# Where three convolution units stand among the matrix products of a fused convolution and feed-forward kernel

## The chip, the cores and the metric

The kernel runs on one core of a Trainium2 chip. The metric is the device time of one execution in microseconds (us); a number of executions is summed up by their median. The core has five engines that run side by side: TensorE (PE; the loads of its stationary operands are listed as PEld), VectorE (DVE), ScalarE (ACT), GpSimd (POOL) and SyncE (SP), which here only issues transfers. Matmul results go to PSUM, a small memory from which VectorE and ScalarE read them.

## The reference

The input x has 8 sequences of 3904 rows with 192 columns. A causal convolution with 7 taps runs along each sequence; the taps are a softmax of the weights, and each of 8 heads (24 columns) has its own. The result goes through a product of two linear maps and two more linear maps:

```python
w = weight - np.max(weight, axis=-1, keepdims=True)
w = np.exp(w)
w = w / (np.sum(w, axis=-1, keepdims=True) + 1e-09)
...
out = np.einsum('hk,bskhg->bshg', w, x_unf)
...
a = x @ w1
b = x @ w2
h = a * b @ w3
return (h @ w_out).astype(np.float32)
```

w1 and w2 are 192 x 1024, w3 is 1024 x 1024, w_out 1024 x 192. The output has 31232 rows of 192 numbers.

## The kernel before

The 31232 rows are cut into two streams of 15616 (`NS`, index `r`), and each stream into 31 chunks of up to 512 rows (`R`). w3 and w_out are multiplied once, early, to one matrix `W_sb` of 1024 x 192, so that per chunk two products are left:

- `first_product(R)` (L581) computes a and b for both streams. For each of 8 blocks of 128 columns (`ft`) PE writes two PSUM tiles, `pa` and `pb`, with 12 matmuls in all, which use the array in halves of 64 rows. ACT casts `pa` to `asb` (L603), DVE multiplies `asb` by `pb` and writes the result to `abT` (L605). The text calls the tiles of ft 6 pa6 and pb6, those of ft 7 pa7 and pb7.
- `second_product(R, r)` (L615) multiplies `abT` by `W_sb` with 32 matmuls on the whole array (L621) into one PSUM tile `ops`; ACT copies it out (L626), SP stores it.

All PSUM tiles come from one pool with four buffers of two banks each (`banks`, L97, L98): each new tile takes the buffer of the tile four before it, whatever its name, and its first write waits until the reader of that older tile is done.

The convolution is done in two ways. For some chunks ("side", L49) it is a sum over taps: ACT makes the first product (`side_first`, L494), DVE adds five more and a last one (`side_sums`, L512), and POOL does some by itself (L539, L559). For the other chunks it is done on PE: `conv` (L310) multiplies rows of x by a small banded matrix `Aband`, with tiles of 32 x 32 of the array. It is called in **units**: one unit is `conv` for two heads of one group of windows `b`, 32 matmuls into two PSUM tiles `cps`, one for each `e`, which alternate in the innermost loops but one (L323 to L331), and are then cast to `convo` (L337). In phases with side sums both casts of a unit are ACT's (`(A, A)`, L836). Twelve units are in the list `units` (L808): four each for the groups 4, 5 and 6, in this order. `convolve(p)` (L834) takes the next unit off the list; after the fourth of a group it stores `convo` to `rows` in DRAM on SP's queue (`store`, L370), from which transposing transfers bring it back to `xT` for later first products. The input of the units, `xb`, is loaded by POOL's queue during first products (L158); where a sequence starts, POOL clears rows of it (L860).

After the start the work goes in **phases** (L725, L863). A phase has the first products of three chunks, then the six second products of three chunks (`ends`). Phase 0 has only second products. Ahead of the six come `side_steps(p, 0, state)` (L897), which puts the first side tap on ACT's queue and sums on DVE's; after each come, in this order, the unit whose place it is, and further side steps. The dictionary `places` (L731) says after which second products, counted from 0, a phase has a unit. Phases 0, 2, 4 and 5 have some: four, four, two and two. In the phases 4 and 5 these are the two halves of group 6.

Of the kernel before, what the change touches and what calls it, by code (L numbers as in the profile page):

```python
# [16 lines left out]
def kernel(  # L17
# [69 lines left out]
    def tok(i):  # L87
        return wins[i][0]
# [33 lines left out]
    def group(r, e):  # L122
        return slice((2 * r + e) * C, (2 * r + e) * C + C)
# [57 lines left out]
    for r in range(NS):  # L181
        p = group(r, 0).start
# [100 lines left out]
    p = group(1, 0).start  # L283
# [26 lines left out]
    def conv(b, c0, wd, evict=(nc.scalar.copy,), es=None):  # L310
        n, m, E = shape_of(b)
        es = range(E) if es is None else es
        if b not in convo_of:
            convo_of[b] = work.tile([128, n, NP, NS, Q], BF16, tag="convo", bufs=2,
                                    name="convo")
            left_of[b] = D * E
        convo = convo_of[b]
        cps = {e: banks("cps") for e in es}
        c = c0
        while c < c0 + wd:  # L320
            h = c // G
            c1 = min(h * G + G, c0 + wd)
            for j in range(4):  # L323
                xb, s = xb_of[b][j]
                for e in es:
                    for r in range(NS):
                        o = cps[e][j * C:j * C + C, r, 0:m * wd]
                        nc.tensor.matmul(  # L328
                            o.rearrange("p (w g) -> p w g", g=wd)[:, :, c - c0:c1 - c0],
                            Aband[group(r, e), h, :], xb[group(r, e), s:s + m, c:c1],  # L330
                            start=True, stop=True)  # L331
            c = c1
        for f, e in zip(evict, es):
            src = cps[e][:, :, 0:m * wd].rearrange("p r (w g) -> p r w g", g=wd)
            o = 0
            for k, lo, c in segments(c0, wd):
                f(out=convo[:, e::E, k, :, lo:lo + c]  # L337
                    .rearrange("p w r g -> p r w g"), in_=src[:, :, :, o:o + c])
                o += c
        left_of[b] -= wd * len(es)  # L340
        if not left_of[b]:
            del xb_of[b]
# [27 lines left out]
    def store(b, first=0, js=range(4)):  # L370
        n = SIZES[b] // 4
        convo = convo_of[b]
        for j in js:
            w = 0
            while w < n:
                i, m = FIRST[b] + j * n + w, 1
                t, s0, s1 = wins[i]
                while w + m < n and wins[i + m] == (t + m * ST, 0, ST):
                    m += 1
                if i < first:  # L380
                    m = first - i
                elif s1 - s0 < ST:
                    m = 1
                    if s1:
                        nc.sync.dma_start(
                            out=rows[t + s0:t + s1, :],
                            in_=convo[C * j + s0:C * j + s1, w].rearrange("s k r g -> s (k r g)"))
                else:
                    src = convo[C * j:C * j + ST, w:w + m].rearrange("s w k r g -> s w (k r g)")
                    dst = rows[t:t + ST * m, :].rearrange("(w s) c -> s w c", s=ST)  # L390
                    for s0, s1 in ((0, 16), (16, ST)):
                        nc.sync.dma_start(out=dst[s0:s1], in_=src[s0:s1])
                w += m
# [28 lines left out]
    def transposes(R, first=0):  # L422
        t0, t1 = max(R * CH, first), min((R + 1) * CH, TS)
        a = ring_of[R] * CH % RING + t0 - R * CH
        for k in range(NP):
            nc.sync.dma_start_transpose(
                out=xT[k][:, a:a + t1 - t0], in_=rows[t0:t1, k * 128:(k + 1) * 128])
# [58 lines left out]
    def side_transpose(i):  # L486
        p, k, t0, t1 = tasks[i]
        for lo, hi in ((t0 - HALO, t0 + CH), (t0 + CH, t1))[:1 + (t1 - t0 > CH)]:
            nc.sync.dma_start_transpose(
                out=raw_of[i % 5 - 1][:, HALO + lo - t0:HALO + hi - t0], in_=rows_c[lo:hi, k, :])  # L490
# [31 lines left out]
    def pool_tiles():  # L522
        t = stage.tile([128, 3 * CH + HALO], BF16, tag="wo", bufs=1, name="acc")
        pool_acc.append(t[:, 0:2 * CH].bitcast(FP32))
        pool_raw.append(t[:, 2 * CH:3 * CH + HALO])
# [202 lines left out]
    def stage_of(R):  # L728
        return R // TRIO

    places = {0: (1, 2, 3, 4), 2: (0, 1, 3, 4), 4: (2, 4), 5: (1, 3)}  # L731
    rooms = (6, 12, 12, 11, 12, 13, 12, 11.25, 12)
    steps = [(i, cost, f) for i in range(len(tasks)) for cost, f in side_sums(i)]
    late_sum = max(v for v, (i, _, _) in enumerate(steps) if tasks[i][:2] == (12, 0))
# [1 line left out]
    starts, chain, begun, room, p = {}, {}, set(), 0, -1  # L736
# [19 lines left out]
    def side_steps(p, n, state):  # L756
        items = chain.get(p, [])
        for v, (i, at, f) in enumerate(items):
            if at is not None and at <= n and v not in state:
                state.add(v)  # L760
                f()
        for v, (i, at, f) in enumerate(items):
            if at is None and v not in state:
                state.add(v)
                f()
            elif v not in state:
                break
# [66 lines left out]
    def convolve(p):  # L834
        b, h, n = units.pop(0)
        conv(b, h * G, n * G, (V, A) if p not in chain or (p == 0 and h >= 2 * n) else (A, A))  # L836
        if h + n == H:
            n = SIZES[b] // 4
            now = [j for j in range(4) if p or tok(FIRST[b] + j * n) < spans[b - 3][0] + CH]
            store(b, js=now)  # L840
            rest.append((b, [j for j in range(4) if j not in now]))
            while sent[0] < len(conv_rounds) and \
                    min((conv_rounds[sent[0]] + 1) * CH, TS) <= spans[b - 3][1]:
                due.append(conv_rounds[sent[0]])
                sent[0] += 1
            for f in results[:4]:
                f()
            del results[:4]
            if p == 0:
                transposes(due.pop(0))  # L850

    def turn(p):
        while due and stage_of(due[0]) <= p + 2 and \
                stage_of(conv_rounds[ring_of[due[0]] - RING // CH]) <= p:
            transposes(due.pop(0))

    def clear():
        for b in list(zero_rows):
            for xb, p0, w in zero_rows.pop(b):
                nc.gpsimd.memset(xb[p0:p0 + PAD, w, :], 0.0)  # L860

    pace = const.tile([1, 2], BF16)
    for p, (rounds, ends) in enumerate(phases):  # L863
        todo = jobs.pop(p, [])

        last = len(points) - 1
        counts = [0] * 3 + [2] * 4 if p == 1 else [2] * 2 + [1] * 5
        at = [[todo.pop(0) for _ in range(min(n, len(todo)))] for n in counts + [len(todo)]]
        if p in places:
            at[last - 1].insert(0, clear)  # L870
        for v, f in enumerate(pool_sum.pop(p, ())):
            at[v].append(f)

        def issue(R, ft, fs):
            def run():
                P(out=pace, in_=abT_of[R][0:1, ft, 1, 0:2])  # L876
                for f in fs:
                    f()
            return run

        for j, R in enumerate(rounds):
            first_product(R, {ft: issue(R, ft, at[v])
                              for v, (a, ft) in enumerate(points) if a == j and at[v]})
        assert not todo
        clear()
        if p == 0:
            pool_tiles()
        turn(p)
        raws = starts.get(p + 1, ())
        late = [i for i in raws if p == 0 or i >= 5 and chain[p][0][0] <= i - 5]  # L890
        for i in raws:
            if i not in late:
                side_transpose(i)
        if p in pool_from:
            pool_transpose(*pool_from[p])
        state = set()
        side_steps(p, 0, state)  # L897
        for n, (R, r) in enumerate((R, r) for R in ends for r in range(NS)):
            if (R, r) == (NR - 1, NS - 1):
                last_product(R, r)  # L900
            else:
                second_product(R, r, results if p == 0 else None)
            if n in places.get(p, ()):
                convolve(p)
            side_steps(p, n + 1, state)
        assert len(state) == len(chain.get(p, ()))
        while results:
            results.pop(0)()
        for b, js in rest:
            store(b, js=js)  # L910
        rest.clear()
        for i in late:
            side_transpose(i)
        turn(p)
# [31 lines left out]
```

## Time and profile before

| what | value |
|---|---|
| median of 3 runs | 511.17 us (510.73 to 512.86) |
| the profiled execution | 510.92 us |
| its span, first to last instruction | 509.2 us |
| granted TensorE clock | 1.00 |
| second products of phase 2 | 148.25 to 166.04 us |
| second products of phase 4 | 244.37 to 261.24 us |
| second products of phase 5 | 292.48 to 309.35 us |

The profile is that of one execution. A row of a timeline has the start in us, the duration in us, the engine, the line of the kernel, the operation, what it writes and reads, and how many instructions are merged in the row; in brackets stand the idle time of the engine ahead of it and what ended that. A row of the table by stage has the stretch, its length, and for each engine its busy time with the number of instructions, then the granted clock, the share of the transfer engines and GB/s. A row of the chain of waits has the start, the time and what set the pace in it; "issue" is time in which the profile shows no cause. PE's busy time counts matmuls that overlap or wait within the array, so a stage of PE is read by the starts of its instructions.

### The profile page before, as it was taken

To read this page: it belongs to the slowest core of one execution; us is meant where nothing else is said; L and a number is where in the kernel's file an instruction comes from. 1 tells how busy PE (TensorE), PEld (TensorE's weight loads), DVE (VectorE), ACT (ScalarE), POOL (GpSimd) and SP (SyncE) were. 2 spreads that over 40 slices of the span, in tenths; PEclk is the share of its full clock that TensorE was granted. 3 is DMA by queue.
4 is the path that set the end of the run, shared out by engine and by line. 5 is a ranking of instruction groups with operands and counts; after the bars stand their busy time and mean duration, and the time that the engine had idled before them with its cause. 6 is when DMAs were issued, how large, how long until landed. Compare 5 with 4: busy or idle time off the path is not lost.

```text
span 509.2 us, 13681 instructions
## 1 busy us (share of the span) xinstructions
PE 503.8 (99%) x5758; PEld 338.5 (66%) x5758; DVE 446.4 (88%) x402; ACT 347.2 (68%) x386; POOL 229.3 (45%) x303
## 2 busy tenths in 40 slices
PE   8999999999999999999999999999999999999997
PEld 4546864595569557845875596569557855965597
DVE  7898769999999799899989999999899999999930
ACT  6786667836778776477667767763776477457752
POOL 9966101333980597079519902970573067100000
PEclk9999999999999999999999999999999999999999
DMA  9999979999955999963889337975501400230024
GB/s 136 158 162 174 173 152 177 148 163 194 159 60 159 143 158 133 229 79 23 65 219 96 24 106 127 192 110 155 102 1 43 156 4 0 84 106 1 1 63 156
DMA packets 156825, 58.45 MB, mean 115 GB/s; under 512 B 112607, under 2 KB 156763, under 8 KB 156763
## 3 DMA queue, kind: packets, MB, share of 16 engines
q0 software_dynamic: 70560, 16.85, 37.2%
q1 hardware_dynamic: 86043, 40.62, 36.1%
q8 instruction: 45, 0.74, 0.6%
q14 instruction: 17, 0.14, 0.1%
q10 hardware_dynamic: 160, 0.10, 0.1%
HBM read 33.97 MB, written 34.85 MB: 135 GB/s over the span
## 4 chain that ended last, share of the span: by engine, by line
PE 98%; DMA 1%; ACT 0%; POOL 0%; DVE 0%; issue 0%; POOLq 0%
PE ops L621 32%; PE pa L596 31%; PE pb L596 31%; PE cps L328 1%; PE wps L693 1%; DMA xb<-in_x_dram 1%; PE tps L401 0%; PE ops L646 0%; PE tps L416 0%; DVE abT L605 0%; PE cps L357 0%; ACT asb L603 0%; POOL xb L158 0%; ACT convo L337 0%; ACT osb L650 0%
## 5 line engine op out<-in xcount | busy, mean ns | idle before, releaser
L605 DVE TENSOR_TENSOR abT<-asb,pb 128x1024 bf16<-128x1024 bf16 x240 | 292.7, 1221 | 30.4 <-ACT asb L603 14.5
L603 ACT CAST asb<-pa 128x1024 bf16<-128x1024 f32 x244 | 247.0, 1012 | 64.2 <-PE pa L596 64.0
L596 PEld LDWEIGHTS <-wn 64*128 64x128 bf16 x1488 | 138.5, 94 | 79.7 <-issue 1.6
L596 PEld LDWEIGHTS <-ws 64*128 64x128 bf16 x1488 | 129.7, 94 | 70.0 <-issue 1.4
L621 PE MATMUL ops<-W_sb,abT 128*128 128x192 bf16 x1936 | 163.7, 246 | 0.0
L621 PEld LDWEIGHTS <-abT 128*128 128x128 bf16 x1936 | 158.5, 98 | 6.4 <-issue 6.4
L596 PE MATMUL pb<-xT,wn 64*128 64x512 bf16 x408 | 111.2, 376 | 0.0
L596 PE MATMUL pa<-xT,wn 64*128 64x512 bf16 x408 | 110.1, 376 | 0.1
L596 PE MATMUL pa<-xT,ws 64*128 64x512 bf16 x408 | 110.1, 376 | 0.0
L596 PE MATMUL pb<-xT,ws 64*128 64x512 bf16 x408 | 108.5, 376 | 0.0
L626 ACT COPY osb<-ops 128x768 f32<-128x768 f32 (+1 forms) x61 | 48.5, 795 | 84.7 <-PE ops L621 82.3
L876 POOL COPY pace<-abT 1x2 bf16<-1x2 bf16 x57 | 10.9, 192 | 175.5 <-DVE abT L605 155.0
L596 PE MATMUL pb<-side,wn 64*128 64x512 bf16 (+1 forms) x336 | 88.8, 368 | 0.0
L596 PE MATMUL pa<-side,ws 64*128 64x512 bf16 (+1 forms) x336 | 87.3, 369 | 0.0
L596 PE MATMUL pa<-side,wn 64*128 64x512 bf16 (+1 forms) x336 | 87.3, 369 | 0.0
L512 DVE SCALAR_TENSOR_TENSOR acc<-raw,wC,acc 128x1024 f32<-128x1024 bf16 (+2 forms) x70 | 84.6, 1209 | 2.0
L596 PE MATMUL pb<-side,ws 64*128 64x512 bf16 (+1 forms) x336 | 85.7, 368 | 0.0
L539 POOL TENSOR_SCALAR tmp<-acc,wC 128x512 f32<-128x512 bf16 x42 | 65.8, 1566 | 1.2
L559 POOL TENSOR_TENSOR acc<-acc,tmp 128x512 f32<-128x512 f32 x35 | 44.4, 1267 | 2.9
L480 POOL DMA_DIRECT2D rows_c<-in_x_dram x50 | 37.1, 744 | 4.7 <-issue 2.7
L158 POOL DMA_DIRECT2D xb<-in_x_dram x50 | 32.2, 649 | 6.9 <-DMA xb<-in_x_dram 2.2
L512 DVE SCALAR_TENSOR_TENSOR acc<-side,wC,acc 128x1024 f32<-128x1024 bf16 (+1 forms) x20 | 24.3, 1217 | 3.8 <-ACT acc L494 3.2
(76 smaller groups left out, 186.9 us busy)
## 6 DMA issues: line engine op xcount, KB each, us to landing
out_dram<-osb SPq DMA_DIRECT2D x54, 384.0 KB
xb<-in_x_dram POOLq DMA_DIRECT2D x16, 240.0 KB, 7.2
out_dram<-osb SPq DMA_DIRECT2D x12, 192.0 KB
rows_c<-in_x_dram POOLq DMA_DIRECT2D x16, 130.0 KB, 5.6
rows_c<-in_x_dram POOLq DMA_DIRECT2D x12, 128.0 KB, 5.7
rows<-convo SPq DMA_DIRECT2D x6, 240.0 KB
xb<-in_x_dram POOLq DMA_DIRECT2D x6, 228.0 KB, 4.9
w3b<-in_moe_w_dram POOLq DMA_DIRECT2D x4, 256.0 KB, 5.5
```

What stands on the lines that cost most here:

```text
L158: nc.gpsimd.dma_start(out=tiles[js[0]][0][group(r, e), s:s + w, :], in_=bass.AP(tensor=x.tensor, offset=(r * TS + t - PAD) * D, ap=[[D, C] ...
L328: nc.tensor.matmul(o.rearrange("p (w g) -> p w g", g=wd)[:, :, c - c0:c1 - c0], Aband[group(r, e), h, :], xb[group(r, e), s:s + m, c:c1], ...
L480: nc.gpsimd.dma_start(out=rows_c[lo:t1, k, r * Q:r * Q + Q], in_=x_rows[r * TS + lo:r * TS + t1, k * Q:k * Q + Q])
L512: nc.vector.scalar_tensor_tensor(out=side_of[p][:, k, o:o + t1 - t0] if last else a, in0=raw[:, HALO + lo - t0 - d:HALO + hi - t0 - d], sc ...
L539: nc.gpsimd.tensor_scalar(out=out, in0=pool_raw[0][:, HALO - d:HALO - d + CH], scalar1=wC[:, k, K - 1 - d:K - d], scalar2=None, op0=ALU.mult)
L559: nc.gpsimd.tensor_tensor(out=a, in0=a, in1=tmp[:, lo - t0:hi - t0], op=ALU.add)
L596: nc.tensor.matmul(p[:, r, f * N:f * N + N], w_of(i, k, r)[rs, ft * 128:(ft + 1) * 128], operand(R, k, rs), start=(k == 0), stop=(k == NP ...
L603: nc.scalar.copy(out=asb[:, :, 0:per * N], in_=pa[:, :, 0:per * N])
L605: nc.vector.tensor_tensor(out=ab[:, f0, :, 0:N], in0=asb[:, :, 0:N], in1=pb[:, :, 0:N], op=ALU.mult)
L621: nc.tensor.matmul(ops[:, g // 2, (g % 2) * D:(g % 2) * D + D], ab[:, jt, r, g * 128:(g + 1) * 128], W_sb[:, jt, :], start=(jt == 0), stop ...
L626: nc.scalar.copy(out=osb.rearrange("p (a g) d -> p a (g d)", g=2), in_=ops[:, 0:ng // 2, 0:2 * D])
L876: P(out=pace, in_=abT_of[R][0:1, ft, 1, 0:2])
```

## The change

A place -1 is brought in: the border between the last first product of a phase and its first second product, behind the side steps that stand there. One unit each of the phases 2, 4 and 5 goes there. Phase 2 has its units after the second products 0, 1, 3 and 4 before, and at -1, 1, 3 and 4 now. Phase 4 has them after 2 and 4 before, and at -1 and 3 now; phase 5 after 1 and 3 before, and at -1 and 2 now. So the other unit of phases 4 and 5 moves forward by one second product. The number of units, their order and their instructions are the same.

```diff
-    places = {0: (1, 2, 3, 4), 2: (0, 1, 3, 4), 4: (2, 4), 5: (1, 3)}
+    places = {0: (1, 2, 3, 4), 2: (-1, 1, 3, 4), 4: (-1, 3), 5: (-1, 2)}
...
         state = set()
         side_steps(p, 0, state)
+        if -1 in places.get(p, ()):
+            convolve(p)
         for n, (R, r) in enumerate((R, r) for R in ends for r in range(NS)):
```

## The prediction

> **What bounds the kernel now.** I read the page's busy times first, then its chain of waits, then a table of busy times by stage, and at the end the single instructions at the places that the change touches.
>
> ```profile
> span 509.2 us, 13681 instructions
> PE 503.8 (99%) x5758; PEld 338.5 (66%) x5758; DVE 446.4 (88%) x402; ACT 347.2 (68%) x386; POOL 229.3 (45%) x303
> PE 98%; DMA 1%; ACT 0%; POOL 0%; DVE 0%; issue 0%; POOLq 0%
> ```
>
> TensorE (PE) is busy for 99% of the span and makes up 98% of the chain that ends last. Nothing that another engine does counts, unless it makes PE wait; and every microsecond by which PE's own sequence gets longer or shorter is one of the whole. So the question is what PE does between two products. The next table has, in order, a stage of first products, a stage of second products without a convolution, the second products of phases 2, 4 and 5 with convolutions, and one second product by itself.
>
> ```profile
> 166.04:197.23 31.19, 31.19 (x290) 15.53 (x290) 27.73 (x23) 24.65 (x25) 25.03 (x29) 1.00 1.09 147
> ...
> 197.23:213.18 15.95, 15.95 (x195) 15.79 (x196) 15.54 (x13) 6.49 (x8) 4.33 (x9) 1.00 1.10 200
> ...
> 148.25:166.04 17.79, 17.79 (x323) 16.35 (x324) 16.98 (x14) 13.53 (x20) 3.52 (x4) 1.00 0.54 133
> 244.37:261.24 16.87, 16.87 (x258) 16.07 (x260) 16.47 (x14) 10.07 (x14) 4.60 (x7) 1.00 0.79 90
> 292.48:309.35 16.87, 16.87 (x259) 16.07 (x260) 16.48 (x14) 11.00 (x15) 0.09 (x1) 1.00 0.45 116
> ...
> 199.98:202.62 2.64, 2.64 (x35) 2.64 (x33) 2.57 (x3) 0.80 (x1) 1.08 (x3) 1.00 1.31 119
> ```
>
> Six second products take 15.95 us. With four units (phase 2) they take 17.79, with two units (phases 4 and 5) 16.87: (17.79 - 15.95) / 4 = 0.46 and (16.87 - 15.95) / 2 = 0.46 us. A unit costs the same wherever it stands between two second products, so today no unit waits for anything: 0.46 us is its work and one more switch of the array. The granted clock is 1.00 throughout.
>
> **What a unit costs, in two parts.** These are PE's rows of phase 2 around its first unit.
>
> ```profile
> 148.19 2.81 PE L621 MATMUL ops<-W_sb,abT 128*128 128x192 bf16 x32
> 150.93 0.42 PE L328 MATMUL cps<-xb,Aband 32*32 32x240 bf16 x32
> 151.29 2.81 PE L621 MATMUL ops<-W_sb,abT 128*128 128x192 bf16 x32
> ```
>
> From the start of the unit's 32 matmuls to the start of what follows is 151.29 - 150.93 = 0.36 us. From one second product's start to the next is 151.29 - 148.19 = 3.10, which is 2.64 + 0.46. So 0.10 of the 0.46 lies ahead of the unit's first matmul, where the array turns from 128 rows to 32. At the border PE pays such a turn today, from the 64 rows of the first product to the 128 of the second:
>
> ```profile
> 243.51 2.52 DVE L605 TENSOR_TENSOR abT<-asb,pb 128x1024 bf16<-128x1024 bf16 x2
> 243.76 1.01 ACT L603 CAST asb<-pa 128x1024 bf16<-128x1024 f32 x1 [0.28 <-PE pa L596]
> ...
> 243.99 0.38 PE L596 MATMUL pb<-xT,wn 64*128 64x512 bf16 x1
> ...
> 244.30 0.92 PE L621 MATMUL ops<-W_sb,abT 128*128 128x192 bf16 x9
> ...
> 25.33 0.38 PE L596 MATMUL pb<-xT,wn 64*128 64x512 bf16 x1
> 25.63 0.40 PE L328 MATMUL cps<-xb,Aband 32*32 32x120 bf16 x32
> 26.12 0.37 PE L596 MATMUL pa<-xT,wn 64*128 64x512 bf16 x1
> ```
>
> From the start of the last matmul of a first product to that of a second product are 244.30 - 243.99 = 0.31 us. Early in the kernel a unit follows directly on a first product, and there it is 25.63 - 25.33 = 0.30: the unit can start where the second product would have started. **Without any wait**, then, the move takes 0.46 out of the later place and puts 0.36 in at the border: 0.10 us less per phase.
>
> **The wait that the move adds.** All matmul results share four buffers in a fixed rotation (line 98). The last two of a first product are pa7 and pb7 (the tiles of ft 7); the next two in the rotation are those that pa6 and pb6 held. Today the first second product takes pa6's, the next one pb6's, 2.64 us later. A unit takes two buffers at once (line 318) and writes the second one with its third matmul (lines 323 to 327). pb6's buffer is free when VectorE's multiply of ft 6 has read it. The two multiplies in the row at 243.51 are those of ft 6 and ft 7 (the second starts as ScalarE's cast of 243.76 ends, 244.77). One takes 1.22 us:
>
> ```profile
> L605 DVE TENSOR_TENSOR abT<-asb,pb 128x1024 bf16<-128x1024 bf16 x240 | 292.7, 1221 | 30.4 <-ACT asb L603 14.5
> ```
>
> So ft 6 is read at 243.51 + 1.22 = 244.73, while PE is ready at 244.30. The trace has the same kind of wait once already. In the chain of waits around 25 us, a unit has taken one buffer out of the rotation, and the pa behind it takes that of the pb two tiles back:
>
> ```profile
> 24.85 1.23 DVE abT L605
> 26.08 0.04 issue
> 26.12 0.82 PE pa L596 x6
> ```
>
> The multiply ends at 26.08, PE goes on 0.04 us later. This is both the rule of the rotation and the price of the signal. At the border of phase 4 the unit's third matmul starts at 244.73 + 0.04 = 244.77, and the second product behind it 0.36 later, at 245.13, against 244.30 today: +0.83. The unit is then missing later: -0.46. Net **+0.37 us**. I take all 0.36 behind the wait, though two of the 32 matmuls go ahead of it; that is 0.02 at most. The other two borders:
>
> ```profile
> 147.40 2.52 DVE L605 TENSOR_TENSOR abT<-asb,pb 128x1024 bf16<-128x1024 bf16 x2
> ...
> 291.62 2.51 DVE L605 TENSOR_TENSOR abT<-asb,pb 128x1024 bf16<-128x1024 bf16 x2
> ...
> 292.41 1.33 PE L621 MATMUL ops<-W_sb,abT 128*128 128x192 bf16 x14
> ```
>
> Phase 2: 147.40 + 1.22 + 0.04 + 0.36 = 149.02 against 148.19, +0.83, net +0.37. Phase 5: 291.62 + 1.62 = 293.24 against 292.41, +0.83, net +0.37.
>
> That the second product stands still behind the waiting unit, though its own buffer (pa7's, cast by 244.77) and its inputs are ready, is the step on which this rests. The page "PSUM — Partial Sum Buffer" of the Trainium skill, section "Engine vs sequencer instructions", says that matmuls start and end in the order of the program. By that rule the sum is the +0.37 above; if the second product could pass, it would be the -0.10 of the case without a wait. No row here shows a matmul held up with a free one behind it, so the trace does not decide.
>
> **What else moves, at nothing, and what covers it.** Phases 4 and 5 shift their other unit forward by one product as well; it stands between second products as before, at 0.46. ScalarE casts a unit's results out:
>
> ```profile
> 148.56 1.15 ACT L494 ACTIVATE acc<-raw,wC 128x1024 f32<-128x1024 bf16 x1
> ...
> 151.73 1.83 ACT L337 CAST convo<-cps 128x960 bf16<-128x960 f32 x2
> ...
> 154.83 1.95 ACT L337 CAST convo<-cps 128x320 bf16<-128x320 f32 x4
> 156.64 1.19 ACT L494 ACTIVATE acc<-raw,wC 128x1024 f32<-128x1024 bf16 x1
> ...
> 164.47 1.28 DVE L512 SCALAR_TENSOR_TENSOR side<-raw,wC,acc 128x1024 bf16<-128x1024 bf16 x1
> 167.94 1.22 DVE L605 TENSOR_TENSOR abT<-asb,pb 128x1024 bf16<-128x1024 bf16 x1 [2.19 <-ACT asb L603]
> ...
> 309.53 1.28 DVE L512 SCALAR_TENSOR_TENSOR acc<-raw,wC,acc 128x1024 f32<-128x1024 bf16 x1
> 311.30 1.22 DVE L605 TENSOR_TENSOR abT<-asb,pb 128x1024 bf16<-128x1024 bf16 x1 [0.49 <-ACT asb L603]
> ```
>
> At the border this cast stands behind the side taps' first pass (148.56 to 149.71) and ends near 151.5; the unit's buffers are wanted again after two second products, at 149.02 + 5.28 = 154.3. 2.8 us cover it. The side sums on VectorE (L512) depend on ScalarE's passes (L494). In phase 2 the second pass slips by 0.37 with PE, and VectorE ends at 165.75 + 0.37 with 2.19 us to spare; in phase 5 there are only 0.49 to spare, but there the unit leaves its place ahead of the second pass, and PE's next first product starts 0.37 later. Nothing comes out of it.
>
> ```profile
> 145.91 0.56 POOL L860 MEMSET xb<- 6x192 bf16 x2
> ...
> 230.14 0.58 POOL L158 DMA_DIRECT2D xb<-in_x_dram  x1
> ...
> DMA to landing us min/median/max: 1.8/7.1/9.2
> ...
> 306.19 4.68 SPq L392 DMA_DIRECT2D rows<-convo  x4
> ```
>
> The unit's input must be there earlier. In phase 2 the last writes to it end at 146.47, 1.7 us ahead of the border. In phase 4 the last load is issued by 230.72 and lands at 239.9 with the slowest landing, 4.4 us ahead. Phase 5 loads nothing new. The stores of phase 5's finished group on SP's queue come one product (2.64 us) earlier, ahead of three output stores instead of two; those wait in their buffers for nothing on PE, and the transposes behind the stores come no later. If that cover were gone, a store's issue of about 1.2 us (4.68 / 4) would hold up an output store only.
>
> **The sum.** 3 x 0.37 = +1.1 us. The profiled run took 510.92 us with 509.2 of span, so 1.7 lie around it; it would take 512.0. It lies 0.25 under the median shown (511.17), so for the median I predict **512.3 us**, span 510.3.
>
> **The rivals.**
> B, no wait on PE: the second product passes the unit, or the multiply of ft 6 is done in time. Each border gives -0.10, together -0.3: 510.9. For it speaks that ft 6's multiply misses by only 0.43 us; against it, that the miss comes out alike at three borders.
> C, slower: the unit gets pa7's and pb7's buffers, not pa6's and pb6's, as it would if the rotation stood two tiles further on at the border. Its third matmul then waits for the multiply of ft 7, which ends at 243.51 + 2.52 = 246.03, and the second product starts at 246.43: +2.13 - 0.46 = +1.67 per phase, +5.0 in all, 516.2. It decides from two tiles more in the rotation. Against it: the code takes none there, and the wait at 26.12 ends with the multiply that the rotation names.
> D, ScalarE's casts hold up the side sums of phase 5 by their 1.95 us: less the 0.49 to spare and the 0.37 of the later PE, +1.1 on top: 513.4. Against it: the unit leaves the place ahead of the second pass.
> A gain of 0.5% has no case here: even three units wholly hidden are 3 x 0.46 = 1.4 us, 509.8.
>
> **How the numbers follow.** About 0.5% (2.6 us: 508.6 to 513.7) is what a measurement of this kernel can tell from no change; its three runs span 510.73 to 512.86. The forecast has 0.63, B 0.13 and D 0.04, all three within that band: same 0.80. C has 0.15: slower. The last 0.05 go to a gain that no view shows: faster. The range: at the bottom B less 0.6 for the spread of the runs, 510.3. At the top the forecast at two borders and C at one, 511.17 + 0.74 + 1.67 = 513.6, and again 0.6: 514.2. It leaves out most of C and of the unseen gain, 0.2 together.
>
> **What would show it.** At the three borders, 32 unit matmuls behind the last pb, of which all but the first two start 0.04 us after the multiply of ft 6 ends; the first second product 0.83 us later than now from the start of the last pb matmul (0.31 becomes about 1.1); the stages of second products 18.2, 17.2 and 17.2 us long; first products unchanged at 31.2. If the stages are shorter than now, the wait is not there (B). If PE waits 1.7 us, it is pb7's buffer (C). If a first product gets longer than 31.3 us, something off PE has slipped (D), and my list of covers is wrong.

## The result and the profile after

Over 16 runs each, the changed kernel has a median of 512.49 us (512.09 to 514.21), the kernel before 511.05 (510.72 to 512.86). The ratio is 1.0028 with a 95% interval of 1.0019 to 1.0037: about 1.4 us slower, within the 0.5% that counted as no change. The profiled span is 510.6 us, against 509.2.

The stages of second products of phases 2, 4 and 5 in the table by stage (stretch, length, busy time of each engine with its instructions, clock, transfers), and the stage of first products ahead of the last:

```profile
148.28:166.67 18.39, 18.18 (x324) 16.69 (x324) 17.02 (x14) 13.53 (x20) 3.55 (x4) 1.00 0.51 129
...
245.00:262.24 17.24, 17.03 (x258) 16.22 (x260) 16.73 (x14) 10.06 (x14) 4.61 (x7) 1.00 0.79 105
262.24:293.49 31.25, 31.25 (x290) 16.60 (x291) 27.73 (x23) 24.69 (x25) 25.08 (x28) 1.00 0.75 101
293.49:310.73 17.24, 17.03 (x258) 16.21 (x260) 16.84 (x15) 11.09 (x15) 0.09 (x1) 1.00 0.50 115
```

They were 17.79, 16.87 and 16.87 us: +0.60, +0.37 and +0.37. PE's busy time is now 0.21 shorter than each stage, where the two agreed before: PE waits once in each. First products are as long as they were. The chain of waits (start, time, what set the pace) names the cause; here it is for the three borders in turn:

```profile
147.44 1.23 DVE abT L605
148.67 0.04 issue
148.71 0.64 PE cps L328 x30
149.34 5.39 PE ops L621 x64
...
244.14 1.23 DVE abT L605
245.37 0.04 issue
245.41 0.42 PE cps L328 x30
245.83 10.67 PE ops L621 x128
...
292.62 1.23 DVE abT L605
293.86 0.04 issue
293.90 0.42 PE cps L328 x30
294.32 2.75 PE ops L621 x32
```

In order they are the multiply of ft 6, 0.04 us until PE goes on, the 30 matmuls of the unit from its first write to pb6's buffer on, and the second product. The chain was PE alone at these places before; now it goes over VectorE's multiply at all three borders, and ahead of that over ScalarE's cast of pa6. In phase 2 the 30 matmuls take 0.64 us, in the others 0.42; this was not foreseen. PE's timeline of phase 2 shows the border in single rows:

```profile
147.92 0.38 PE L596 MATMUL pb<-xT,wn 64*128 64x512 bf16 x1
148.22 0.28 PE L328 MATMUL cps<-xb,Aband 32*32 32x240 bf16 x2
148.71 0.64 PE L328 MATMUL cps<-xb,Aband 32*32 32x240 bf16 x30 [0.21 <-DVE abT L605]
149.28 0.34 PE L621 MATMUL ops<-W_sb,abT 128*128 128x192 bf16 x2
```

From the start of the last pb matmul to the start of the second product are 149.28 - 147.92 = 1.36 us; the same rows give 1.15 and 1.14 at the other borders, where the kernel before has 0.30 to 0.31. Below, this distance is called the border. Less the old border and the 0.46 that a unit no longer takes later, the three come to +0.59, +0.38 and +0.38, together 1.35 of the 1.4 us between the spans.

### The profile page after: what moved, and what is told of

Same layout as the page of the kernel before. It is cut to its first block, busy times and chain, and to the rows that moved or that the text cites. A ratio compares the mean times of both kernels' runs of the same rounds, so it can differ in the third digit from the quotient of the medians.

```text
span 510.6 us, 13682 instructions
## 1 busy us (share of the span) xinstructions
PE 505.0 (99%) x5758; PEld 339.4 (66%) x5758; DVE 446.2 (87%) x402; ACT 347.3 (68%) x386; POOL 229.4 (45%) x303
## 4 chain that ended last, share of the span: by engine, by line
PE 96%; ACT 1%; DVE 1%; DMA 1%; POOL 0%; issue 0%; POOLq 0%
PE ops L621 32%; PE pa L596 31%; PE pb L596 30%; PE cps L328 1%; PE wps L693 1%; DVE abT L605 1%; DMA xb<-in_x_dram 1%; ACT asb L603 1%; PE tps L401 0%; PE ops L646 0%; PE tps L416 0%; PE cps L357 0%; POOL xb L158 0%; ACT convo L337 0%; ACT osb L650 0%
## 5 line engine op out<-in xcount | busy, mean ns | idle before, releaser
L605 DVE TENSOR_TENSOR abT<-asb,pb 128x1024 bf16<-128x1024 bf16 x240 | 292.7, 1221 | 31.2 <-ACT asb L603 15.3
```

What stands on the lines that cost most here:

```text
L605: nc.vector.tensor_tensor(out=ab[:, f0, :, 0:N], in0=asb[:, :, 0:N], in1=pb[:, :, 0:N], op=ALU.mult)
```

## The experiments

Each is one profiled run. The time until the first second product of phase 0 (52.08 us before) differed by up to 1.5 us among these runs, in stages that no edit touches; so stages and borders are compared, and spans only where that start is alike.

**Free pb6's buffer.** The changed kernel; in the last chunk ahead of each of the three borders the multiply of ft 6 reads `asb` in place of pb6, so a factor of the result is left out there:

```diff
+                other = asb if f0 == 6 and R in (8, 14, 17) else pb
                 nc.vector.tensor_tensor(out=ab[:, f0, :, 0:N], in0=asb[:, :, 0:N],
-                                        in1=pb[:, :, 0:N], op=ALU.mult)
+                                        in1=other[:, :, 0:N], op=ALU.mult)
```

> The changed kernel, but in the last chunk of phases 2, 4 and 5 the multiply of ft 6 multiplies asb by itself and reads pb6 no more, so pb6's buffer is free as soon as PE has written it (it leaves out the factor b for these three blocks). Theory W (PE waits at the border for the multiply that reads pb6, and the second product stands behind): from the start of the last pb matmul to the first of the second product 0.30 + 0.36 = 0.66 us at all three borders (changed kernel: 1.36, 1.15, 1.14), span 509.2 - 3 x 0.10 = 508.9. Rival T (the turn from 64-row to 32-row tiles costs it): the three borders as in the changed kernel, span 510.6. The 0.21 more at the border of phase 2: 0.66 there if it is two semaphore waits that queue behind the wait for pb6, 0.87 if the unit itself is longer there.

The span was 510.8, but its first second product came at 53.55, 1.5 us late. The borders were 0.83, 0.83 and 0.82: neither the 0.66 that was expected nor the 1.14 to 1.36 of the changed kernel. PE's timeline, a row of VectorE's and the chain of waits of this run at phase 2:

```profile
149.34 0.38 PE L596 MATMUL pb<-xT,wn 64*128 64x512 bf16 x1
149.65 0.42 PE L328 MATMUL cps<-xb,Aband 32*32 32x240 bf16 x32
150.17 0.49 PE L622 MATMUL ops<-W_sb,abT 128*128 128x192 bf16 x4
...
148.86 1.06 DVE L606 TENSOR_TENSOR abT<-asb 128x1024 bf16<-128x1024 bf16 x1
...
149.11 1.02 ACT asb L603
150.13 0.04 issue
150.17 1.89 PE ops L622 x21
```

The unit no longer waits: its 32 matmuls stand in one row without idle time. The replaced multiply itself runs until 148.86 + 1.06 = 149.92, past the unit's start, and in phase 5 it does so too (until 294.72, with the unit at 293.97); in phase 4 it ends at 245.71, 0.10 ahead of the unit. So the unit waits for the reader of pb6 and not for the multiply as such, and the turn of the array did not cost that time. But behind the unit the second product now waits, for another thing: its own buffer is pa7's, and ScalarE's cast of pa7 ends at 150.13. There were two waits, one hidden behind the other. Phase 2 is alike with the rest here: its extra time has gone with the wait.

**Free pa7's buffer as well.** In addition, ScalarE's cast of ft 7 reads the `asb` of ft 6 in these three chunks, so that pa7 is left out too:

```diff
-            nc.scalar.copy(out=asb[:, :, 0:per * N], in_=pa[:, :, 0:per * N])
+            src = asb_last if f0 == 7 and R in (8, 14, 17) else pa
+            nc.scalar.copy(out=asb[:, :, 0:per * N], in_=src[:, :, 0:per * N])
+            asb_last = asb
```

> As the run in which pb6 is not read by the multiply of ft 6, and in addition ScalarE's cast of ft 7 in these chunks reads the asb of ft 6 in place of pa7 (it leaves out these blocks of the result). The border of 0.83 that was left there ended with the cast of pa7, whose buffer the second product takes. Theory W with both waits: 0.30 + 0.36 = 0.66 us at all three borders, stages of second products 0.10 us shorter than in the kernel before (17.7, 16.8, 16.8). Rival: 0.83 again, and the 0.17 belong to the turn from 64-row over 32-row to 128-row tiles.

PE's timeline of this run, phase 2:

```profile
147.91 0.38 PE L596 MATMUL pb<-xT,wn 64*128 64x512 bf16 x1
148.22 0.42 PE L328 MATMUL cps<-xb,Aband 32*32 32x240 bf16 x32
148.58 0.67 PE L624 MATMUL ops<-W_sb,abT 128*128 128x192 bf16 x6
```

0.67, and 0.66 at the other two. This is the price of the move without any wait: 0.31 + 0.46 - 0.67 = 0.10 us saved per phase. The stages agree: from their first matmul to the next first product they take 17.68, 16.76 and 16.76, against 17.78, 16.87 and 16.87 in the kernel before. The span of 509.0 shows only 0.2 of the 0.3, because a later stage of first products, which no edit touches, took 31.47 instead of 31.24; why is not shown. With the price of 0.66 the changed kernel's border is accounted for: 0.66 for the work and the turns, 0.17 more for the cast of pa7, 0.32 more for the multiply that reads pb6, and in phase 2 another 0.21.

**One tile after the other.** In the unit at the border, all matmuls into the tile with the free buffer first, then those into the tile that waits:

```diff
+        for part in ([[e] for e in es] if split else [es]):
...
-                for e in es:
+                    for e in part:
```

> The changed kernel, but the unit at the border does all 16 matmuls into its first tile (whose buffer is free) and then the 16 into its second. Theory W: the first half goes into the time of the wait; what is left behind it falls from 0.36 to 0.20 to 0.30 us, so the borders of phases 4 and 5 are 0.99 to 1.09 us instead of 1.15; phase 2 falls as much from 1.36 (its two semaphore waits still come behind the wait); span 510.1 to 510.4. Rival T: nothing falls, or the border gets longer, since only half of the array's tiles work at a time: 510.6 or more.

Borders 1.34, 1.12 and 1.12: only 0.02 to 0.03 less, well under what was expected. PE's timeline at phase 2 (the row spans the wait), then the chain of waits at phase 2 and phase 4:

```profile
148.42 1.10 PE L329 MATMUL cps<-xb,Aband 32*32 32x240 bf16 x32
...
148.90 0.62 PE cps L329 x16
149.52 0.52 PE ops L622 x5
...
245.58 0.40 PE cps L329 x16
245.98 4.07 PE ops L622 x48
```

Half of the matmuls stand behind the wait now, and they take 0.40 us in the chain, where 30 took 0.42. Each half uses 8 of the array's 16 tiles of 32 x 32, with two matmuls on each, one per head; the whole unit uses all 16, also with two on each. The trace's records of single matmuls at phase 4 show it: the 16 matmuls behind the wait start in two groups of 8, at 245.58 and 245.69, and in the changed kernel the 30 behind the wait start in two groups too, at 245.41 and 245.51. Half as many matmuls take as long, so almost nothing is won by moving the other half into the wait. The order inside the unit is no way out. Phase 2's 0.22 us more are still there.

**The other tile first.** The same with the two tiles in the other order:

```diff
-        cps = {e: banks("cps") for e in es}
+        order = list(es)[::-1] if split else es
+        cps = {e: banks("cps") for e in order}
-        for part in ([[e] for e in es] if split else [es]):
+        for part in ([[e] for e in order] if split else [es]):
```

> As the run with one tile first, but the border unit does the other tile (e = 1) first, in the free buffer, and e = 0 second, in pb6's. In phase 2 the matmuls on e = 1 are those with the two extra semaphore waits of PE's queue, which now come ahead of the wait for pb6. Theory Q (the 0.21 more at phase 2's border are these two waits, 51 ns each on the sequencer and what they hold up, queued behind the wait): phase 2's border falls from 1.34 to 1.12 us, those of phases 4 and 5 stay at 1.12. Rival U (the first unit of a group is longer by itself at a border, whatever the order): phase 2 stays at 1.34. Span 510.3 by Q in an undisturbed run, 510.5 by U.

Borders 1.12, 1.12 and 1.12. The chain at phase 2, then the row for the semaphore instructions among the units' matmuls on PE's queue (count, durations in ns, start of the first and the last), of this run, the changed kernel, the run that freed pb6, and the kernel before, in this order:

```profile
148.95 0.40 PE cps L330 x16
...
L330 PEldq EVENT_SEMAPHORE  x5: 51/51/51, 4.7 to 147.9; - x5
```

```profile
L328 PEldq EVENT_SEMAPHORE  x5: 51/51/51, 4.7 to 148.9; - x5
```

```profile
L328 PEldq EVENT_SEMAPHORE  x5: 51/51/51, 4.7 to 149.0; - x5
```

```profile
L328 PEldq EVENT_SEMAPHORE  x5: 51/51/51, 4.7 to 150.3; - x5
```

In the changed kernel the last two of them stand behind the first matmul that waits, and run after its release, at 148.73 and 148.85. The records of single matmuls show PE held up by each: eight matmuls start from 148.71 to 148.73, the next one at 148.83, and the others not before 148.96. In this run the last one comes at 147.9, ahead of the last matmul of pb7 (148.16) and of the wait; in the run with pb6 free at 149.0, ahead of the last matmul of pb7 there (149.34); in the kernel before at 150.3, ahead of the unit (150.93). In none of the three does it cost anything. The two instructions wait for semaphores of two loads of xb, which had landed by 135.6: phase 2's unit is the first to touch that input, and two of its matmuls need three waits each, while no matmul and no weight load in this trace carries more than one; the third is such an instruction. Phase 4's unit is the first of its group too, but it has no semaphore instruction (the last of the five stands in phase 2). So theory Q, the two waits queued behind the wait for pb6, holds; rival U, that the unit is longer by itself, does not.

**The rest of the shift.** The kernel before, with only the other units of phases 4 and 5 moved:

```diff
-    places = {0: (1, 2, 3, 4), 2: (0, 1, 3, 4), 4: (2, 4), 5: (1, 3)}
+    places = {0: (1, 2, 3, 4), 2: (0, 1, 3, 4), 4: (2, 3), 5: (1, 2)}
```

> The kernel before, but with the other unit of phases 4 and 5 one place forward as in the change (4: after 2 and 3, 5: after 1 and 2); nothing at the border. Theory W: nothing, span 509.2, second products of phases 4 and 5 at 16.87 us each. Rival S (the shift of these units, their casts or the earlier stores cost part of it): 0.2 us or more on the second products or on the first products behind them, span 509.4 to 510.

The table by stage of this run, second products of phases 2, 4 and 5:

```profile
148.38:166.17 17.79, 17.79 (x323) 16.35 (x322) 17.10 (x14) 13.60 (x20) 3.64 (x4) 1.00 0.55 134
244.49:261.36 16.87, 16.87 (x259) 16.07 (x258) 16.47 (x14) 10.14 (x14) 4.74 (x7) 1.00 0.85 92
292.60:309.47 16.87, 16.87 (x259) 16.07 (x258) 16.48 (x14) 11.07 (x15) 0.22 (x1) 1.00 0.48 112
```

These are the 17.79, 16.87 and 16.87 of the kernel before, and the first products behind them take 31.19 and 31.24, also as before. The span is 509.4, 0.2 longer, and its first second product came 0.2 later (52.27). Moving these units, their casts and the stores costs nothing.

**Phase 2 as before.** The changed kernel with only the two later borders:

```diff
-    places = {0: (1, 2, 3, 4), 2: (-1, 1, 3, 4), 4: (-1, 3), 5: (-1, 2)}
+    places = {0: (1, 2, 3, 4), 2: (0, 1, 3, 4), 4: (-1, 3), 5: (-1, 2)}
```

> The changed kernel with phase 2 as before: units at the border in phases 4 and 5 alone. The costs of the three borders add up if each is a wait of its own: second products of phase 2 17.79 us, of phases 4 and 5 17.24, span 509.2 + 2 x 0.37 = 509.9. If phase 2's border shifted what the later phases find (transfers, side sums), phases 4 and 5 would differ from 17.24 by 0.1 us or more.

The border is 0.31 in phase 2, as in the kernel before, and 1.14 in phases 4 and 5, as in the changed kernel. The span was 510.8, with a start 0.8 us late (52.89); less that it is 510.0. The borders add up one by one.

**Two units at the border.** Phases 4 and 5 with both of their units there:

```diff
-    places = {0: (1, 2, 3, 4), 2: (-1, 1, 3, 4), 4: (-1, 3), 5: (-1, 2)}
+    places = {0: (1, 2, 3, 4), 2: (0, 1, 3, 4), 4: (-1, -1), 5: (-1, -1)}
...
-        if -1 in places.get(p, ()):
+        for _ in range(places.get(p, ()).count(-1)):
             convolve(p)
```

> Phase 2 as before; phases 4 and 5 with both of their units at the border. Theory W: the second unit takes pa7's and pb7's buffers, so its third matmul waits for the multiply of ft 7; the second product then takes the first unit's first buffer and waits until ScalarE has cast it, behind the cast of pa7 and the side taps' first pass: about 2.7 us from the last pb matmul to the second product, +1.45 per phase against the kernel before, span about 512.1. Rival T (cost of the turn, paid once for two units): about 1.4 us, +0.2 per phase, span 509.5.

The borders were 2.73 and 2.78 us. PE's timeline at phase 4, and the end of the chain of waits there:

```profile
244.83 0.38 PE L596 MATMUL pb<-xT,wn 64*128 64x512 bf16 x1
245.14 0.28 PE L328 MATMUL cps<-xb,Aband 32*32 32x240 bf16 x2
245.62 0.43 PE L328 MATMUL cps<-xb,Aband 32*32 32x240 bf16 x32 [0.21 <-DVE abT L605]
246.92 0.42 PE L328 MATMUL cps<-xb,Aband 32*32 32x240 bf16 x30 [0.86 <-DVE abT L605]
247.56 0.66 PE L621 MATMUL ops<-W_sb,abT 128*128 128x192 bf16 x6 [0.22 <-ACT convo L337]
...
245.51 1.15 ACT acc L494
246.66 0.86 ACT convo L337
247.52 0.04 issue
247.56 1.48 PE ops L621 x16
```

The whole rotation can be read here. The first unit waits for ft 6. The second unit's first two matmuls go along with it (into pa7's buffer), its third waits for ft 7, 1.30 us later. Then the second product, whose turn in the rotation is the first unit's first tile, waits until ScalarE has cast that one, behind the side taps' pass. The 2.7 us expected were met; the rival's 1.4 were not.

**The other border.** The kernel before, with the last unit of each of the three phases behind the last second product:

```diff
-    places = {0: (1, 2, 3, 4), 2: (0, 1, 3, 4), 4: (2, 4), 5: (1, 3)}
+    places = {0: (1, 2, 3, 4), 2: (0, 1, 3, 5), 4: (2, 5), 5: (1, 5)}
```

> The kernel before, with the last unit of phases 2, 4 and 5 at the other border: behind the last second product, ahead of the next phase's first product. The turns of the array are as many as with the unit at the first border (0.10 us less per phase than between second products). Theory W, carried over: the buffers are free there, but ScalarE's casts of the unit (1.8 to 1.95 us) come ahead of its cast of the next pa, and VectorE's multiply and the buffers of the first blocks follow that: PE waits 0.9 to 1.3 us in each of the next first products, span 511.5 to 513. Rival T (only the turns count): span 508.9, a version faster than both.

The span was 512.7, within what was expected. The chain of waits after phase 2:

```profile
166.21 0.44 ACT convo L337
166.65 0.41 issue
167.06 0.98 ACT convo L337
168.04 0.93 ACT asb L603
...
169.04 1.23 DVE abT L605
170.28 0.04 issue
170.32 0.82 PE pb L596 x6
```

ScalarE casts the unit's two tiles, and only then the first pa; the multiply is late by that, and PE stands before a pb whose buffer the multiply holds. Here too the turns alone would have paid about 0.10 per phase: the second products of phase 4 with their units, up to the next first product, took 16.76 instead of 16.87. Neither border has room for a unit, and no version among these that computes the whole result beats the kernel before.

## Why the prediction was right, and where it was off

*The wait for pb6's buffer.* As predicted, in place, cause and size: the third matmul starts 0.04 us after the multiply of ft 6 ends, and the borders of phases 4 and 5 cost +0.38 and +0.38 where +0.37 was worked out. Freeing the buffer took the wait away; the unit's other tile, and a second unit, waited just for what the rotation names.

*Phase 2.* "+0.83, net +0.37" was a term too small: it measured +0.59. The 0.36 between the unit's start and the second product was read from a place where PE's queue runs ahead of the array, so two semaphore waits of that unit (the last at 150.3, the unit at 150.93) cost nothing there. Behind a waiting matmul they cost 0.21 to 0.22. This is the larger part of the difference between the predicted span (510.3) and the measured one (510.6).

*The case without a wait.* "0.10 us less per phase" is right as the price of the turns (0.66 to 0.67 measured with both buffers free). As the price of rival B, in the form that the multiply of ft 6 is done in time, it was wrong: had the multiply of ft 6 been in time, the second product would still have waited for pa7's cast, with a border of 0.83, and the move would still have cost 0.83 - 0.31 - 0.46 = +0.06 per phase. The prediction had the row (the cast ends at 244.77, after 244.30 + 0.36 = 244.66) and used it only to show that this buffer was ready in time behind the longer wait.

*The second product held up behind the unit.* It starts when the unit is through. The prediction had no row of a matmul held up with a free one behind it; the changed kernel now has one, inside the unit. Of its 32 matmuls 16 write the tile whose buffer is free, but only the two that stand ahead of the first waiting one start at 148.22; the other 14 start with or after the release at 148.71. With all 16 put first, they start at 148.42 to 148.55, ahead of the release at 148.90. So these matmuls start in the order of the program, and in that the trace agrees with the rule that the prediction takes from the Trainium skill's page "PSUM — Partial Sum Buffer", section "Engine vs sequencer instructions". For the second product itself no run shows it: the cast of its own buffer ended at 148.70, hardly after the multiply (148.67), so it was not free any earlier.

*The covers.* They held: the other units' shift costs nothing (16.87 in both), first products stay at 31.2, and no load, no cast of a unit and no side sum shows in the chain at the three borders. D did not occur. C did not either; the run with two units shows that its wait, for the multiply of ft 7, meets the unit that stands two tiles later.

## What to carry to other kernels

A border between two stages is not an idle place just because the engine changes its work there: the last buffers of the first stage are still being read, and work that takes several buffers at once meets readers that the next stage, with one buffer at a time, does not. Before moving work across a border, write down for each of its buffers who read it last and when, and do so for the work behind it too, since a second wait may hide behind the first. A cost that was read where the queue runs ahead of the engine need not hold where the queue has to wait.

## What the runs showed of the hardware that was not expected

Two semaphore waits of 51 ns on PE's queue, for loads that had long landed, held PE up by 0.21 us when they were queued behind a matmul that waits, and cost nothing when the queue was ahead. And 16 matmuls on 8 tiles of 32 x 32 took 0.40 us in the chain, while 30 on all 16 tiles took 0.42: in both cases each tile works through two.
